# A recurrent attention stage ahead of a routed expert layer: seven idle products of 128 columns in place of fourteen of 64

## The chip, the cores and the metric

The kernel runs on one core of a Trainium2 chip. The metric is the device time of one execution in microseconds; the time of a kernel is the median of its runs. Inputs and outputs are float32.

## What is computed

A gated linear recurrence over 4 x 8 heads, 768 steps and 48 channels makes 3072 rows of 384 numbers; each row then goes to the one of 8 experts whose embedding it is closest to.

```python
for t in range(S):                       # B, H, S, D = 4, 8, 768, 48
    state = alpha[:, :, t, :, None] * state + np.einsum('bhd,bhe->bhde', k[:, :, t], v[:, :, t])
    y[:, :, t] = np.einsum('bhd,bhde->bhe', q[:, :, t], state)
x = y.transpose(0, 2, 1, 3).reshape(B * S, H * D)        # 3072 x 384
logits = xn @ en.T / tau                 # xn, en: rows scaled to length 1
expert_idx = np.argmax(logits, axis=1)
gate_w = probs[np.arange(N), expert_idx] # softmax of the logits
for e in range(E):                       # E = 8, w1: 384 x 1024, w2: 1024 x 384
    mask = expert_idx == e
    h = np.maximum(x[mask] @ w1[e], 0.0)
    out[mask] = gate_w[mask, None] * (h @ w2[e])
```

## The kernel before

The sequence is cut into 24 chunks of 128 steps (six for each of the four batches). The recurrent stage is one loop over the chunks (L719), software-pipelined: in turn s it loads chunk s + 2, decays chunk s, scores chunk s - 1, mixes chunk s - 2 and makes rows of chunk s - 3. Then come the expert layers, which are long chains of products.

At the start `warm(14)` (L713, the function at L684) issues fourteen products of the identity matrix with its own first 64 columns, into a PSUM tile `pw` that nobody reads. They need only `ident`, which POOL makes first. Then `fixed_parts` (L222) fills the constant parts of the buffers on POOL and DVE, `load(0)` (L447) issues the loads of chunk 0 on SP's queue, and `prepare_loads` (L262) issues a few small ones on ACT's. `load(s)` brings the decays `at` in two transfers (L453), the keys `kt` (L454), the queries `qt` (L455), and the values `vt` of chunk s - 1 (L458). There are four buffers of each of the first three and five of the values. Each transfer is made of runs of 192 bytes, 48 numbers.

Within a chunk the order is this. `turned` (L433) transposes the decays on TensorE, four blocks of 128 x 128, into the PSUM tile `pa`; `decays` (L467) scans them backward on DVE into `r` (L480), transposes the keys into `pk`, multiplies both into `kr` (L487), and transposes the queries into `pq`. `queries` (L491) copies `pq` to `qc` on ACT (L496). `decay_queries` (L498) scans `pa` forward on DVE into `a` (L509), and POOL multiplies `qc` and `a` into `qs` (L513). In the next turn `keys_back` (L521) transposes `kr` back into `pkb`, `scores` (L565) multiplies `qs` and `kr` into `sc`, and `update` (L542) makes the next state.

The tiles `pa`, `pk`, `pq` and `pkb`, and a small `p0` of the first chunk (the starts of the decays, which `prepare_first` transposes), take turns in three PSUM buffers (`ps_tr`); `pw` uses the one buffer of `ps_mm`, which later serves `pd` and `px`. Each engine runs its instructions in the order in which the program lists them. `in_turn` keeps TensorE's order that of the code: the idle products, then pa, pk, pq of chunk 0, p0, pkb of chunk 0, then pa of chunk 1. `mm` (L191) and `tr` (L194) are helpers that issue every product and transpose of this stage, so the profile gives those lines (L192, L195) for them, and the tiles tell them apart.

After the last chunks SP fetches the rows that the first expert was sent (`fetch_early`, L176) and the weights (`weights`, L134 on), which need to know which expert comes first.

Of the kernel before, what the change touches and what calls it, by code (L numbers as in the profile page):

```python
# [9 lines left out]
FP32 = mybir.dt.float32  # L10
# [17 lines left out]
def kernel(  # L28
# [16 lines left out]
    P = 128  # L45
# [9 lines left out]
    HALF = P // 2  # L55
# [21 lines left out]
    ident = consts.tile([P, P], FP32)  # L77
# [113 lines left out]
    def mm(*args, **kwargs):  # L191
        last["pe"] = nc.tensor.matmul(*args, **kwargs)  # L192
# [8 lines left out]
    with ExitStack() as c1:  # L201
# [5 lines left out]
        ps_mm = c1.enter_context(tc.tile_pool(name="ps_mm", bufs=1, space=PSUM))  # L207
# [14 lines left out]
        def fixed_parts():  # L222
            for i in range(NBUF):
                nc.gpsimd.memset(at_s[i][:, :, D:DP], 1.0)

                nc.gpsimd.memset(at_s[i][0:1], 0.0)
                nc.vector.memset(kt_s[i][:, :, D:DP], 0.0)
                nc.vector.memset(qt_s[i][:, :, D:DP], 0.0)
                if i == 0:
                    nc.gpsimd.memset(inr, 0.0)  # L230
                    for p in range(NP - 1):
                        nc.gpsimd.memset(inr[:, p * P + P - 1 : (p + 1) * P], 1.0)
                    for j in range(NR):
                        nc.vector.memset(r_s[j][:, NP * P - 1 :], 1.0)
                if i < 2:
                    nc.vector.memset(ini_s[i], 0.0)
            make_upper_triangular(nc, causal[:, 0], val=1.0, diag=True)
            for i in range(NBV):
                nc.vector.memset(vt_s[i][:, :, D:DP], 0.0)
# [443 lines left out]

        def warm(n):  # L684

            pw = ps_mm.tile([P, HALF], FP32, tag="mm", name="pw")
            for _ in range(n):
                mm(pw, lhsT=ident, rhs=ident[:, 0:HALF], start=True, stop=True)

        send = []  # L690
        placed_at = {}
# [18 lines left out]
            return n  # L710

        lead = []
        warm(14)  # L713
        fixed_parts()
        load(0)
        a0 = prepare_loads()
# [712 lines left out]
```

## Time and profile before

| | us |
|---|---|
| median of 3 runs | 405.84 |
| lowest and highest run | 404.31, 406.27 |
| the profiled execution | 416.3 |
| its span, first to last instruction | 414.6 |

| engine | busy, us | share of the span |
|---|---|---|
| PE (TensorE products) | 398.9 | 96% |
| PEld (TensorE weight loads) | 354.6 | 86% |
| DVE (VectorE) | 259.3 | 63% |
| POOL (GpSimd) | 252.7 | 61% |
| ACT (ScalarE) | 205.4 | 50% |

The profile is of one execution, which was slower than the runs that were not profiled. PE's busy time is modelled, since products are pipelined: it says that products were under way, not that TensorE worked at its peak rate. The page cuts the span into 40 slices of some 10.4 us; the recurrent stage takes the first 13, the choice of experts and the first weights two or three more, the experts the rest. TensorE's clock can be granted in full or in part; the record of the clock in the trace begins at 15.14 us, and the views show the time before it as full clock although the instructions there have twice the length of later ones of the same kind.

### The profile page before, as it was taken

What the parts mean: (1) busy time and instruction counts of PE and PEld (TensorE: products, weight loads), DVE (VectorE), ACT (ScalarE), POOL (GpSimd) and SP (SyncE); (2) the same over time, 40 slices, a digit from 0 to 9 for tenths busy, and PEclk for the clock granted to TensorE, in tenths of its full rate; (3) what the DMA queues carried; (4) which work ended last, traced back from release to release, by engine and by line L of the source; (5) the groups of instructions that cost most, each with busy time, mean ns of one, the idle gap of its engine ahead of it and who ended that gap; (6) DMA issues with size and microseconds to landing.
All of it is one profiled execution on the core that took longest, in us unless ns stands there. A gap on an engine that the chain in (4) does not pass through costs nothing. (4 is left out here: it accounts for less than half of the span.)

```text
span 414.6 us, 12189 instructions
## 1 busy us (share of the span) xinstructions
PE 398.9 (96%) x4688; PEld 354.6 (86%) x4688; DVE 259.3 (63%) x655; ACT 205.4 (50%) x516; POOL 252.7 (61%) x344
## 2 busy tenths in 40 slices
PE   8999999999999989999999999999999999899994
PEld 8889989888898768588979979989979979879974
DVE  4999979788889514792583572680582375374640
ACT  3455545554455532653673753662672482492520
POOL 6365687677766434771837939937837755946301
PEclk9999999999999996999999999999999999999998
DMA  9999999998986992495802903703800910100101
GB/s 140 155 166 155 155 185 188 195 193 157 191 174 125 344 371 86 136 344 180 290 16 68 344 19 115 291 19 94 315 20 21 337 50 19 40 2 16 40 16 45
DMA packets 119539, 60.26 MB, mean 145 GB/s; under 512 B 102447, under 2 KB 113976, under 8 KB 119472
## 3 DMA queue, kind: packets, MB, share of 16 engines
q1 hardware_dynamic: 115368, 49.15, 50.2%
q0 software_dynamic: 3728, 10.16, 6.9%
q8 instruction: 44, 0.72, 0.7%
q14 instruction: 23, 0.19, 0.2%
q10 hardware_dynamic: 376, 0.05, 0.1%
HBM read 49.69 MB, written 11.45 MB: 147 GB/s over the span
## 5 line engine op out<-in xcount | busy, mean ns | idle before, releaser
L990 DVE TENSOR_TENSOR hT<-hT,pq 128x384 f32<-128x384 f32 x84 | 45.5, 553 | 50.9 <-PE pq L1098 31.3
L860 POOL DMA_INDIRECT out_dram<-y,sx x25 | 24.6, 983 | 65.9 <-ACT y L995 42.4
L513 POOL TENSOR_TENSOR qs<-qc,a 128x512 f32<-128x512 f32 x24 | 30.6, 1276 | 37.0 <-DVE a L509 15.9
L1098 PE MATMUL pq<-xT_m,w_m 128*128 128x192 f32 x252 | 45.4, 326 | 0.0
L973 PE MATMUL pyo<-w,hT 128*128 128x384 f32 x128 | 42.6, 486 | 0.0
L1098 PEld LDWEIGHTS pq<-xT_m,w_m 128*128 128x128 f32 x252 | 40.8, 190 | 0.0
L973 PEld LDWEIGHTS pyo<-w,hT 128*128 128x128 f32 x128 | 24.0, 190 | 14.8
L312 POOL DMA_INDIRECT xs<-x,dest x24 | 24.2, 1009 | 17.8 <-DVE x L656 10.1
L480 DVE TENSOR_TENSOR_SCAN r<-pa,inr 128x511 f32<-128x511 f32 x24 | 29.2, 1216 | 9.0 <-PE pa L195 8.6
L995 ACT ACTIVATE hT<-hT 128x384 f32<-128x384 f32 x56 | 28.4, 518 | 12.2 <-DVE hT L990 9.6
L1010 POOL TENSOR_TENSOR w_m<-w 128x768 f32<-128x768 f32 x12 | 22.6, 1883 | 17.4 <-PE pq L1195 17.4
L1052 POOL TENSOR_TENSOR w_m<-w,w_m 128x256 f32<-128x256 f32 x42 | 30.1, 729 | 3.8 <-PE pq L1098 2.4
L192 PE MATMUL sc<-qs,kr 64*64 64x128 f32 x768 | 29.4, 273 | 2.1 <-issue 2.1
L509 DVE TENSOR_TENSOR_SCAN a<-pa,ini 128x512 f32<-128x512 f32 x24 | 29.3, 1223 | 1.1
L1195 PE MATMUL pq<-w_m,hT_m 128*128 128x192 f32 x168 | 28.5, 327 | 0.2 <-issue 0.2
L1052 POOL TENSOR_TENSOR w_m<-w 128x256 f32<-128x256 f32 x36 | 26.3, 742 | 3.7 <-PE pq L1098 2.4
L1195 PEld LDWEIGHTS pq<-w_m,hT_m 128*128 128x128 f32 x168 | 27.4, 190 | 0.5 <-issue 0.5
L192 PEld LDWEIGHTS sc<-qs,kr 64*64 64x64 f32 x768 | 22.7, 134 | 4.6 <-issue 4.2
L192 PE MATMUL pyx<-sm,vt 128*64 128x128 f32 x384 | 26.3, 279 | 0.0
L652 ACT COPY lg<-pyx 128x32 f32<-128x32 f32 x24 | 4.4, 185 | 40.8 <-PE px L192 34.7
L192 PEld LDWEIGHTS pyx<-sm,vt 128*64 128x64 f32 x384 | 20.5, 136 | 4.1 <-issue 3.6
L624 ACT COPY ycols<-pyx 128x256 f32<-128x256 f32 x48 | 17.9, 377 | 9.4 <-PE pyx L192 5.9
(230 smaller groups left out, 1003.6 us busy)
## 6 DMA issues: line engine op xcount, KB each, us to landing
w<-in_moe_w_dram SPq DMA_DIRECT2D x12, 1536.0 KB
kt<-in_k_dram SPq DMA_DIRECT2D x24, 192.0 KB
qt<-in_q_dram SPq DMA_DIRECT2D x24, 192.0 KB
vt<-in_v_dram SPq DMA_DIRECT2D x24, 192.0 KB
xg<-xs SPq DMA_DIRECT2D x22, 196.5 KB
at<-in_alpha_dram SPq DMA_DIRECT2D x24, 168.0 KB
w<-in_moe_w_dram SPq DMA_DIRECT2D x6, 512.0 KB
w<-in_moe_w_dram SPq DMA_DIRECT2D x8, 384.0 KB
```

Of the source, the lines that this page charges most:

```text
L192: last["pe"] = nc.tensor.matmul(*args, **kwargs)
L312: ins = nc.gpsimd.indirect_dma_start(out=xs, out_offset=bass.IndirectOffsetOnAxis(ap=rows, axis=0), in_=x, in_offset=None, bounds_check=E ...
L480: nc.vector.tensor_tensor_scan(r[:, L - 2 :: -1], pa[:, L - 1 : 0 : -1], inr[:, L - 2 :: -1], 1.0, ALU.mult, ALU.add,)
L509: d["a_scan"] = by_dve = nc.vector.tensor_tensor_scan(a, pa, ini, 0.0, ALU.mult, ALU.add)
L513: by_pool = nc.gpsimd.tensor_tensor(qs.rearrange("p n t -> p (n t)"), d["qc"], a, ALU.mult)
L860: ins = nc.gpsimd.indirect_dma_start(out=out, out_offset=bass.IndirectOffsetOnAxis(ap=col, axis=0), in_=y, in_offset=None, bounds_check=N - 1,
L973: pe[:] = [nc.tensor.matmul(py, lhsT=hT[:, f], rhs=w2_t[:, f], start=(f == 0), stop=(f == FT - 1),)]
L990: dve[:] = [call(*args, **kwargs)]
L995: act[:] = [call(*args, **kwargs)]
L1052: by(w[to], w[x], w[y], op)
L1098: pe[:] = [nc.tensor.matmul(to[:, f], lhsT=w[left][:, f * P : (f + 1) * P], rhs=x[right], start=start and f == 0, stop=stop, skip_group_ch ...
L1195: pe[:] = [nc.tensor.matmul(to, lhsT=left[:, f], rhs=right[:, f], start=start and f == 0, stop=stop and f == n - 1, skip_group_check=True,)]
```

## The change

`warm` multiplies the identity with all of its 128 columns instead of its first 64, into a tile of 128 columns, and is called with 7 instead of 14. The number of columns that pass through is the same, 896; the number of products, and so of weight loads, is half. TensorE's other instructions, and those of all other engines, keep their number and their order.

```diff
         def warm(n):
 
-            pw = ps_mm.tile([P, HALF], FP32, tag="mm", name="pw")
+            pw = ps_mm.tile([P, P], FP32, tag="mm", name="pw")
             for _ in range(n):
-                mm(pw, lhsT=ident, rhs=ident[:, 0:HALF], start=True, stop=True)
+                mm(pw, lhsT=ident, rhs=ident, start=True, stop=True)
...
         lead = []
-        warm(14)
+        warm(7)
         fixed_parts()
         load(0)
         a0 = prepare_loads()
```

## The prediction, made before the changed kernel was run

> **What bounds the kernel now.** I read the page first (times of the engines, the 40 slices), then the chain of waits, then the timeline of the first 30 us, and the waits in that stretch. The chain of waits follows only the last 32 us, so it can't say what the start is worth; the start has to be read from the timeline.
>
> The page says that the recurrent stage (the first 13 of 40 slices, some 135 us) keeps DVE and the loads busy together:
>
> ```profile
> PE   8999999999999989999999999999999999899994
> DVE  4999979788889514792583572680582375374640
> DMA  9999999998986992495802903703800910100101
> DMA packets 119539, 60.26 MB, mean 145 GB/s; under 512 B 102447, under 2 KB 113976, under 8 KB 119472
> ```
>
> What counts is the first digit of DVE, 4, before a row of 9s: DVE begins late. The timeline (start, duration, engine, line, operation, count, idle time before and its releaser) says why:
>
> ```profile
> 1.55 6.23 PE L192 MATMUL pw<-ident 128*128 128x64 f32 x28 [1.55 <-POOL ident masks.py:199]
> ...
> 7.58 1.06 PE L195 MATMUL pa<-ident,at 128*128 128x128 f32 x4
> ...
> 8.43 1.06 PE L195 MATMUL pk<-ident,kt 128*128 128x128 f32 x4
> 8.75 1.22 DVE L480 TENSOR_TENSOR_SCAN r<-pa,inr 128x511 f32<-128x511 f32 x1 [4.74 <-PE pa L195]
> ...
> 10.07 0.69 DVE L487 TENSOR_TENSOR kr<-pk,r 128x512 f32<-128x512 f32 x1
> ...
> 10.89 1.22 DVE L509 TENSOR_TENSOR_SCAN a<-pa,ini 128x512 f32<-128x512 f32 x1
> ...
> 17.51 0.60 PE L195 MATMUL pa<-ident,at 128*128 128x128 f32 x4
> ```
>
> The first chunk's transposes (pa) stand on PE straight behind the idle products (pw), and DVE waits 4.74 us for pa. Did pa wait for its data? The chunk's decays come in two transfers; the last landing records of their semaphores stand at 3.77 and 4.01 us. So for 3.3 us the data lay there and PE was busy with products nobody reads: the warm-up sets the start, not the load.
>
> From 8.75 us on DVE has hardly a gap: in the waits of the first 30 us the row of r is 5.0 us in two waits, 4.7 of it this first one.
>
> ```profile
> DVE r L480 <- PE pa L195: 5.0, 2, 4.7
> ```
>
> The scan r starts at 8.75, 13.50, 18.15 and 22.59 us: about 4.6 us a chunk. DVE's own work per chunk, from the same rows, is 1.22 (r) + 0.69 (kr) + 0.17 + 1.22 (a) + 0.67 (mask) + 0.41 (state) + 0.27 = 4.65 us. So the stage is paced by DVE, and whatever moves the first r moves the stage, unless the loads stop it.
>
> **What the Trainium skill says.** "TensorE: Matmul & The Clock Gate", Part 1, says that TensorE runs at half clock until about 3.4 us of sustained activity, counted in a free-running window. The trace agrees about the two rates (four transposes: 1.06 us at 7.58, 0.60 at 17.51), but PE is counted busy from 1.55 us and the clock record turns full only at 15.14; products of 64 columns evidently didn't count as enough. Part 4 of the page says that transposes don't count as activity; the trace contradicts it: the 3.4 us before 15.14 held almost nothing else. The section on LDWEIGHTS prices a load by its columns (128 / 1.2 = 107 ns, with no word on f32); here the pitch of a 64-column pass is twice that, so I take the measured pitch. "DMA: Bandwidth & Descriptors", Specifications, wants 512 B per transfer for full rate; here 102447 of 119539 packets are smaller, and the early slices move 140 to 190 GB/s where weight slices reach 344.
>
> **The change, part by part.** *Price of a pass.* An f32 product is two passes: 14 products are the 28 records. Their start-to-start time is (6.23 - 0.42) / 27 = 0.215 us with the first, 0.2134 without it. Does the weight load or the stream of columns set it? Transposes at half clock stream 128 columns behind a load of 128, and have the same pitch: (1.06 - 0.42) / 3 = 0.213. At full clock the start-to-start times in the trace are 323 ns for 384 columns (L973), 163 for 192 (L1098), 112 for 128 (L961): proportional to the columns. So at half clock 64 columns take some 107 ns of stream, 128 some 213, and the load of 128 fills up to 213 beside it. A pass of 128 columns therefore still takes 0.213 us. Bounds: 0.224 (twice 112), and 0.32 if load and stream added up (107 + 213), which the transposes exclude.
>
> *Sum.* 28 passes become 14: 14 x 0.2134 = 2.99 us less PE time (at 0.224: 2.83; at the excluded 0.32: 1.5). PE is free for pa at 7.58 - 2.99 = 4.59 us. The decays landed at 4.01, so pa is still behind the warm-up, by 0.6 us, and gets all of the 2.99. DVE's fills end at 4.0 and hide nothing more.
>
> *What follows in chunk 0.* r starts at 8.75 - 2.99 = 5.76. kr needs pk, whose load landed at 5.60: pk runs 5.65 to 6.71, and r ends at 6.98, so kr keeps the 2.99. pq's load lands at 6.67, so pq gains only 2.4; its copy qc stands behind a square root on ACT that ends at 8.05 and comes at about 8.1 to 8.6. The product qs on POOL waits for the scan a, at about 9.1, so that is hidden. But the backward transposes pkb(0) wait for the PSUM buffer that qc frees: about 8.75 in place of 11.37, 2.6 earlier, and pa(1) stands behind them. At half clock pa(1) then begins at 9.65 and r(1) at 10.8, 2.7 earlier; at full clock r(1) is held by DVE's small product L292, which ends with POOL's qs as before, and keeps 3.0.
>
> *The clock.* With 128 columns the passes are stream without pause. Over the window of 1.48 to 4.90 us (15.14 less three windows of 3.413) I estimate 97% stream where before it was 50%; windows of 67% did not open the gate before, one of 96% did. So the gate probably opens at about 5 us, and at other phases of the window by about 7. That shortens pa by up to 0.3 us. Afterwards PE is waiting for loads in chunk 0 and may fall back for a window or two; then it is as cold as before. I book the clock at nothing, 0 to +0.3 us for r, and -0.3 for the pkb detour.
>
> *What is late next: the loads.* They run by their own queue (SP), filling from 0.8 us on at 160 GB/s, and don't come sooner. Slack between landing and use before: decays 4.0, 4.4, 4.0, 5.1, 4.1 us for chunks 1 to 5; keys 3.8, 3.9, 3.4, 3.2, 3.8; queries 3.4, 3.2, 2.9, 2.6, 3.1, later 3.3 and more, from chunk 10 over 5. A shift of 2.99 takes nearly all of that. Only queries of chunks 3 and 4 come late, by 0.1 and 0.4 us, and their product isn't needed until scan a ends 3 us later. So the loads let 2.6 to 3.0 pass.
>
> *Later.* The expert weights are fetched at 133.4 us and from 134.3, behind scattered rows; 3 us earlier is 131.3, and the last load of the recurrent stage landed at 130.7, so they don't collide. The expert stage follows from these. Nothing is added that anything waits for.
>
> Sum: -2.99, with -3.3 and -2.6 as ends. The profiled execution's 416.3 us (span 414.6, 1.7 around it) would become 413.3, span 411.6. The runs' median is 405.84, 10.5 us under the profiled one; the shift is in PE passes and carries over as it is: **402.8 us**.
>
> **The rivals.**
> A, the load front (chance 0.17): the 3 us are given back to the loads. For it: slack of 2.6 to 4 us in ten chunks, and DMA share over 1 all through. Against it: slack grows to 7 us by chunk 15, so the late chunks are paced by compute. If the unprofiled runs have the loads already at the front, only some 0.5 is left: 405.3.
> B, more than the shift (0.08): the early full clock also shortens chunks 0 and 1, half of some 6 us of PE work at half rate, of which DVE hides most; I give it 1.5 us: 401.3. Against it: DVE was 0.9 busy from 8.75 us on.
> C, slower (0.08): a clock relapse. Running at the load front, PE stands still inside chunks and the gate falls to half. The record of the clock shows one such fall, at 155.1 us, for 6.8 us, after a window with about 30% stream. In the recurrent stage PE streams 90% of a window, so such a fall costs up to 0.9 x 3.4 = 3.1 us more PE time, DVE hiding none once PE is late; two falls cost 6.2, less the 3.0 gained: 409. It decides from two falls on. Against it: a window with 59% stream (141 us) did not bring it down, and stops of a few tenths don't reach that.
> D, the change doesn't do what it says (0.03): passes of 128 columns cost 0.32 and nothing else: 1.5 us less, 404.3.
>
> **How the numbers follow.** The main case has 0.64: 402.8, its own range 402.2 to 404.0. Runs of the kernel before scatter from 404.31 to 406.27, so about 1 us of that goes to each side. Range: 401.0 (B, less scatter) to 405.2 (A nearly whole); C and the rest of A stay out. 0.5%, about what a measurement of this kernel can tell from no change, is 2.0 us: faster is under 403.8. Main case 0.90 of 0.64, B whole, D a third: 0.67. Same: the rest of the main case, A and D: 0.25. Slower: C: 0.08.
>
> **What would show it.** Right: 14 records of pw ending near 4.6 to 4.8 us, pa directly behind them, r at 5.4 to 5.9, idle before r under 2 us, later r starts 2.6 to 3.3 us earlier, the weights' first fetch near 131.3, and a clock record that turns full before 8 us. Wrong: pa waiting for a load; r(5) at 33.9 as before (A); further half-clock stretches before 130 us (C); 0.32 us between passes (D).

## The result, and the profile after

The changed kernel is no faster. Its median was 407.12 us (404.57 to 410.44, 20 runs) against 405.68 for the kernel before (402.92 to 407.99, 20 runs): a ratio of 1.0053, 95% interval 1.0031 to 1.0076. Two later comparisons gave 1.0000 (0.9972 to 1.0027) and 1.0006 (0.9988 to 1.0025), so the small loss of the first did not come back; what stands is that 3 us saved at the start were not seen at the end.

The profiled execution after took 409.06 us, span 407.3, where that of before took 416.3. These two must not be subtracted. The later runs were on three chips: on two of them the kernel before takes about 414 us (before_again to w14x128 on the one, stage_before to after_wlate on the other), on the third about 405 (first_before to light_after). One mark in the traces tells the two kinds apart, two waits of some 3 us on ACT in turns 9 and 13, which are shown further down: all twelve traces from the 414 us chips have them, none of the six from the 405 us chip has. By this mark the profile shown of the kernel before is of the first kind, although the runs beside it took 405.84 us, and the profile after is of the second. More than the change lies between them.

The start is what the prediction said. The timeline of the changed kernel (start, duration, engine, line, operation, count, idle time before and its releaser):

```profile
1.55 3.36 PE L192 MATMUL pw<-ident 128*128 128x128 f32 x14 [1.55 <-POOL ident masks.py:199]
...
4.70 0.66 PE L195 MATMUL pa<-ident,at 128*128 128x128 f32 x4
...
5.47 1.22 DVE L480 TENSOR_TENSOR_SCAN r<-pa,inr 128x511 f32<-128x511 f32 x1 [1.47 <-POOL sel L256]
...
6.26 0.63 PE L195 MATMUL pk<-ident,kt 128*128 128x128 f32 x4 [0.89 <-DMA kt<-in_k_dram]
...
7.23 0.63 PE L195 MATMUL pq<-ident,qt 128*128 128x128 f32 x4 [0.34 <-DMA qt<-in_q_dram]
```

Fourteen passes take 3.36 us where 28 took 6.23; pa follows directly, and r starts at 5.47 instead of 8.75 (pa ended at 5.36; the view names POOL, which ended a small fill in between). But pk and pq, which stood behind products before, now stand behind transfers. That goes on: in the waits of the recurrent stage (8 to 135 us; total, count, longest) there is now a line which the kernel before lacks in its profile altogether.

```profile
PE pq L195 <- DMA qt<-in_q_dram: 4.7, 7, 1.5
```

The page's slices show both. DVE begins with 7 instead of 4, PE with 6 instead of 8.

```profile
PE   6899999989999999989999999989999999999994
DVE  7898988788989436962762762671581484474640
DMA  9999989999999993867306506404701900100101
DMA packets 119539, 60.26 MB, mean 148 GB/s; under 512 B 102447, under 2 KB 113976, under 8 KB 119472
```

The row of DMA says less than it seems to. Of the first 13 slices, which are the recurrent stage, twelve are 9 and one is 8, where the profile of before had 8, 9, 8, 6 in slices ten to thirteen. But the transfers were busy nearly all the time in both (their share from 68 to 129 us is 0.99 against 0.96), the bytes and packets are the same, and the two profiles are of different kinds of chip. Which work waited for transfers is told by the waits.

### The profile page after: what moved, and what is told of

Read it like the earlier page. It is cut to its first block, busy times and chain, and to the rows that moved or that the text cites. A ratio compares the mean times of both kernels' runs of the same rounds, so it can differ in the third digit from the quotient of the medians.

```text
span 407.3 us, 12161 instructions
## 1 busy us (share of the span) xinstructions
PE 387.6 (95%) x4674; PEld 344.0 (84%) x4674; DVE 257.9 (63%) x655; ACT 205.9 (51%) x516; POOL 254.0 (62%) x344
## 5 line engine op out<-in xcount | busy, mean ns | idle before, releaser
L860 POOL DMA_INDIRECT out_dram<-y,sx x25 | 24.6, 982 | 65.5 <-ACT y L995 43.7
L1052 POOL TENSOR_TENSOR w_m<-w 128x256 f32<-128x256 f32 x36 | 27.6, 778 | 4.5 <-PE pq L1098 2.2
L192 PE MATMUL sc<-qs,kr 64*64 64x128 f32 x768 | 25.9, 271 | 0.0
L1010 POOL TENSOR_TENSOR w_m<-w,w_m 128x768 f32<-128x768 f32 x12 | 21.9, 1821 | 0.6
L1202 DVE SCALAR_TENSOR_TENSOR y<-pq,gt,u 128x192 f32<-128x192 f32 x21 | 8.7, 415 | 20.4 <-PE pq L1195 18.8
```

Of the source, the lines that this page charges most:

```text
L860: ins = nc.gpsimd.indirect_dma_start(out=out, out_offset=bass.IndirectOffsetOnAxis(ap=col, axis=0), in_=y, in_offset=None, bounds_check=N - 1,
L1010: by(to, x, y, ALU.subtract)
L1052: by(w[to], w[x], w[y], op)
```

## The experiments

A whole-kernel comparison is good to about 1 us, so the search went by kernels that end early, some of which scatter less, and by the start of DVE's scan r in chunks 0, 5, 12 and 23, read from the timelines; r(5) stands for the scan of chunk 5. Each such start comes from one profiled execution. Differences of medians are between two kernels that ran beside each other on the same chip. The absolute times in the first four expectations are those of the first comparison, which was on a faster chip.

### The change again, and its two parts apart

The kernel before once more, the changed one, and two crossings. In w7x64:

```diff
-        warm(14)
+        warm(7)
```

and in w14x128, beside the wider tile, `warm(14)` is left as it was.

before_again: 

> The kernel before, unchanged, once more. Theory 1 (the profile shown of before was not like its usual runs: its clock opened only at 15.1 us and fell once more at 155 us): this profile has a span near 404 us, its clock record turns full before 10 us, the idle products end before 7.0 us, and there is no half-clock stretch near 155 us. Theory 2 (every run of before is like the one shown, and the changed kernel loses some 4 us elsewhere that it had won at the start): the clock turns full near 15 us, the idle products end at 7.6 to 7.8 us and DVE's first scan starts at 8.75 us. Ratio to before 1.000 within 0.3% under both.

after_again: 

> The changed kernel, once more. Theory 1 (the start is 1 to 2 us earlier than in a usual run of before, and the loads take it back): first scan at 5.4 to 5.8 us, queries used within 0.2 us of their landing in several of the first ten chunks, clock full at 5 to 7 us, median 406 to 408, span 404 to 407. Theory 2: the same start, but a half-clock stretch or a longer expert stage in the profile that the usual runs of before don't have.

w7x64: 

> Seven idle products of 64 columns: as long as the changed kernel's at half clock (14 passes, 3.0 us) but with half of the columns. If the early start is what costs (PE and DVE at the load front), it is as slow as the changed kernel, 406 to 408. If the early full clock is what costs, the clock opens later here (after 8 us) and the time is that of before or under, 404 to 406. If a late clock is what costs, it is the slowest, over 408.

w14x128: 

> Fourteen idle products of 128 columns: as much PE time as before at half clock, with twice the columns, so the clock should open at about 5 us and the products end at about 6.3 us instead of 7.6. If the early start costs, this is between before and the changed kernel, 405.5 to 407. If the early full clock costs, it is as slow as the changed kernel, 407. If neither does, it is as before, 405.7.

On a chip where the kernel before takes 414.23 us, the four took 414.26, 414.05, 414.34 and 413.53 us (ratios 0.9993, 1.0000, 1.0003, 0.9982, each within 0.3% either way). In their traces r(0) starts at 8.76, 5.62, 5.77 and 8.10 us. So r(0) moved by 3.0 to 3.1 us with seven products, wide or narrow, and the time of the whole by at most 1.2 us by the intervals. The passes' form is not the cause: seven narrow ones, which end as early, bring as little.

### How far the gain comes: kernels ended early

stage_before and stage_after end behind the recurrent stage and the choice of experts: no expert weights, no early first layer and no expert layers. early_before and early_after keep the weights of the first two experts and the first layer that runs beside the last chunks. Core of the edits:

```diff
-    with ExitStack() as c3:
...
+    nc.sync.dma_start(out=out[0:P], in_=blank[:, 0:DM])
```

stage_before: 

> The kernel before cut to the recurrent stage and the choice of experts with its scattered rows: the expert weights' loads, the first expert's early layers and all expert layers are left out, and one block of the output is written. Alone it is the reference for the next run. Expected from the profiles of before: about 150 us plus what lies around the span.

stage_after: 

> The same cut with seven idle products of 128 columns. Theory A (the stage itself gives the early start back to the loads): 0 to 1 us under the cut of before. Theory B (the stage keeps some 2 us, as the two profiles of the same chip show at the last chunk, 132.2 against 134.1 us, and something behind it takes them): 1.5 to 2.5 us under the cut of before.

early_before: 

> The kernel before up to the end of the choice of experts, with the weights of the first two experts loaded and the first expert's early first layer; all later expert layers are left out, and one block of the output is written. Reference for the next run; about 175 us.

early_after: 

> The same with seven idle products of 128 columns. Theory A: 0 to 1 us under its reference. Theory B1 (the early first layer takes the gain, waiting for weights that come no sooner): the cut without weights gains 1.5 to 2.5 us, this one 0 to 1. Theory B2 (the gain is lost in the expert layers): this one gains 1.5 to 2.5 us as well.

early_before_2: 

> The cut up to the early first layer, from the kernel before, a second time (its six runs scattered from 174.0 to 179.0 us). Theory B1 (the early first layer and the weights take the gain): the next run is 0 to 1 us under this one. Theory B2 (the gain passes this part and is lost in the expert layers): 1.5 to 2.5 us under it.

early_after_2: 

> The same cut with seven idle products of 128 columns, a second time. B1: 0 to 1 us under its reference, with PE standing still for 1 us or more inside the last chunk's scores, where the kernel before has none; B2: 1.5 to 2.5 us under, and no such stop.

The stage took 163.75 and 161.54 us: some 2 us of the gain are still there when it ends, on a chip of the 414 us kind. With the early layer the two pairs differ by 0.5 and 2.5 us (175.29 and 174.77, 176.47 and 174.00); over all 25 runs it is 1.5 ± 1.4 us. The first pair alone would have said "lost here", the second "kept": one pair of six runs each could not decide it.

In the traces of this kind of chip r(0), r(5), r(12), r(23) start at 8.76, 33.87, 71.36, 134.11 (before_again) and 5.62, 32.03, 69.46, 132.18 (after_again). Of the 3.1 us, 1.3 are given up in the first five chunks (0.9 in the pair of stage kernels), nothing later. In the two pairs with the early layer the lead at r(23) is 1.6 us.

What lies beside the last chunks is the weights' stream. In early_after the last chunk's 32 scores stop before the last two, for 1.33 us in which PE waits for nothing that the profile shows ("issue"); the first product with the weights (phe) comes behind them:

```profile
137.97 1.05 PE L192 MATMUL sc<-qs,kr 64*64 64x128 f32 x29
...
140.35 0.38 PE L192 MATMUL sc<-qs,kr 64*64 64x128 f32 x2 [1.33 <-issue]
140.65 1.56 PE L192 MATMUL phe<-exT,w 128*128 128x256 f32 x6
```

From the first of the scores to the last it is 0.88 us in the kernels that start late (before_again, w14x128, both early_before), and 1.75 to 2.57 in the early ones on these chips (after_again, w7x64, early_after, early_after_2); without any weights (stage_after) it is 0.97. Over all traces with weights the stop goes with one thing: it is there in the five in which the first weights were issued 0.4 to 1.8 us ahead of r(23) (these four and light_after, below), and in none of those in which they were issued at most 0.14 us ahead of it or behind it. In the three pairs here the lead of 1.6 to 1.9 us at r(23) has shrunk to 0.8 (after_again), -0.1 and 0.2 us at the first phe. Without a stop PE is not free of the weights either: in before_again it stands at phe for them, for 0.6 us.

### The weights held back

The first weights' load was made to wait for a small fill of its first column on POOL, placed behind the masks of the last chunk but one (the call of `weights(0)` that stood ahead of it is taken out):

```diff
+            if s == NS - 1:
+                with tc.issue_after(st[NS - 2]["masked"].ins):
+                    nc.gpsimd.memset(w1_s[0][:, 0, 0:1], 0.0)
+                with tc.issue_after(v_last.ins):
+                    weights(0)
```

early_after_wlate: 

> The cut with seven idle products of 128 columns, and the first expert's weights held back by a small fill of their first part behind the mask of chunk 22, so that their stream begins about 1.7 us later and stands to the compute as in the kernel before. If the weights' early stream causes the stop inside the last scores[...], the stop goes, and the cut is 1 to 2 us faster than the one without the hold. If the stop has another cause, it stays, and the time is the same or slower by up to 1 us (weights later).

after_wlate: 

> The whole changed kernel with the same hold on the weights. If the weights' early stream is what took the gain: 1.5 to 2 us under the kernel before. If the gain is lost in the expert layers or in the scatter of runs: within 1 us of the kernel before.

The hold was longer than meant: the weights were issued at 137.38 us, 5 to 6 us later rather than 1.7. The stop in the scores is gone (0.88 us again, in after_wlate too), so it comes with the weights' early stream. But the first product with these weights begins at 140.81, no sooner than in the early kernels without the hold (140.65 and 140.15), because it now waits for them:

```profile
140.81 0.67 PE L192 MATMUL phe<-exT,w 128*128 128x256 f32 x2 [2.81 <-DMA w<-in_moe_w_dram]
```

The rest of the stream is late too: 181.32 us against 174.00 (early_after_2), 420.07 for the whole kernel (1.0156, 1.0102 to 1.0210). As a remedy it fails; as a reading it shows that early weights cost a stop and late ones a wait.

### Past the first expert, on the other kind of chip

first_before and first_after end after the first of the eight experts; after_3 is the changed kernel again; after_hold has a shorter hold, by a fill on DVE ahead of r(23).

```diff
-        for i in range(E):
+        for i in range(1):
...
-        run_rest((E - 1) % NW)
```

first_before: 

> The kernel before, ended after the first of its eight experts (the other seven, and the last scatter of their rows, are left out). Theory 1 (the gain of the start is lost inside the choice and the first expert, where the weights' stream and the late semaphore counts lie): the median of first_before stands within 0.6 us of that of first_after. Theory 2 (the gain of 1.5 to 2.2 us is still there behind the first expert and goes in the seven later ones): first_before is longer by 1.5 us or more. About 205 to 215 us in all.

first_after: 

> The changed kernel, ended after the first of its eight experts in the same way. Theory 1: within 0.6 us of first_before. Theory 2: 1.5 to 2.2 us under it. If it is longer than first_before by over 0.6 us, the first expert gives back more than the start brings.

after_3: 

> The changed kernel once more. If its time against the kernel before depends on the chip (1.0053 in the first comparison, 1.000 in the second), then on a chip where the kernel before takes about 414 us it is again within 0.3% of it; if the two comparisons differ by scatter alone, this one may fall anywhere from 0.998 to 1.005.

after_hold: 

> The changed kernel with the weights of the first two experts held back by a small fill on DVE ahead of the last chunk's r, so that they are issued about as far ahead of r(23) as in the kernel before. If the early weights' stream is what takes the gain away (it stops PE inside the last chunk's scores for 1 to 1.6 us), the stop falls to 0.9 us and the time is 1 to 2 us under after_3, 412 to 413. If the stop only stands in the place of the wait for the same weights, phe begins when it did or later, and the time is that of after_3 within 0.6 us, or up to 2 us more.

This chip was of the 405 us kind (405.10 for the kernel before), like that of the first result. Medians: 191.75 and 190.37 for the two that end after the first expert, or 1.5 ± 1.5 us by all eleven runs, which lies between the two theories and decides neither; 405.40 for after_3 (ratio 1.0006); 404.91 for after_hold (0.9984, 0.9962 to 1.0007). In after_hold the fill came too early to hold anything: the weights were issued at 128.73 us, as in after_3 at 128.83. It tells nothing of the stream, and no version here beats the kernel before.

The traces tell more than the times. The start of r in the four chunks:

| us | r(0) | r(5) | r(12) | r(23) |
|---|---|---|---|---|
| first_before | 8.74 | 34.19 | 70.45 | 130.02 |
| first_after | 5.86 | 31.40 | 67.68 | 129.30 |
| after_3 | 5.85 | 31.80 | 68.15 | 128.82 |
| after_hold | 5.87 | 31.95 | 68.22 | 128.54 |

The lead of first_after is 2.9, 2.8, 2.8 and then 0.7 us: on this kind of chip most of it is lost between chunks 12 and 23. The other two traces of early kernels lose less there, 1.1 and 0.8 us, and more before. The waits of that stretch (68 to 135 us) name a taker, first in first_after, then in first_before (after_3 has 1.3 us in this row, after_hold 0.8):

```profile
PE pq L195 <- DMA qt<-in_q_dram: 2.2, 3, 1.0
```

```profile
PE pq L195 <- DMA qt<-in_q_dram: 0.7, 2, 0.4
```

One such wait in first_after's timeline, in chunk 12, with what stands behind it:

```profile
69.01 0.42 PEld L195 LDWEIGHTS pq<-ident,qt 128*128 128x128 f32 x4 [1.17 <-issue]
69.04 0.63 PE L195 MATMUL pq<-ident,qt 128*128 128x128 f32 x4 [0.97 <-DMA qt<-in_q_dram]
...
70.48 1.06 PE L192 MATMUL sc<-qs,kr 64*64 64x128 f32 x32
...
71.29 0.63 ACT L496 COPY qc<-pq 128x512 f32<-128x512 f32 x1
...
71.99 1.27 POOL L513 TENSOR_TENSOR qs<-qc,a 128x512 f32<-128x512 f32 x1 [2.50 <-ACT qc L496]
```

PE runs its products in the order of the code, so the scores of the chunk before, which need nothing of these queries, come late as well; the turn takes 6.38 us instead of 5.23. Even first_before has no room left at the end: the queries of chunks 19, 21, 22 and 23 land 0.1 us ahead of their first weight load.

Why does the profile of before, on which the prediction rests, show no such wait? There, and in before_again, some turns of the late chunks are longer for another reason: r(9) to r(10) is 6.88 us and r(13) to r(14) 6.90, where first_before has 5.63 and 5.40. The waits of 45 to 135 us in the profile of before:

```profile
ACT lg L652 <- remote: 6.1, 2, 3.1
...
PEld sc L192 <- issue: 3.9, 8, 0.6
...
PE sc L192 <- issue: 2.1, 7, 0.4
```

The first is ACT waiting for small products (px; "remote" says that the view finds nothing on this core that ended the wait): in turn 9 the last of them ends at 55.74 us and ACT goes on at 57.46, where in first_before it goes on 0.05 us behind them. The last px and the wait, first in before, then in first_before:

```profile
55.52 0.22 PE L192 MATMUL px<-sel,ycols 64*64 64x56 f32 x1
57.46 0.18 ACT L652 COPY lg<-pyx 128x32 f32<-128x32 f32 x1 [3.06 <-remote]
```

```profile
55.83 0.22 PE L192 MATMUL px<-sel,ycols 64*64 64x56 f32 x1
56.09 0.19 ACT L652 COPY lg<-pyx 128x32 f32<-128x32 f32 x1 [1.38 <-PE px L192]
```

The other two are stops of PE inside the scores. None of the three is there in first_before or in after_3. The longer turns leave the loads more time: the decays of chunks 12 to 23 lie ready for 7.4 us on average in the profile of before (6.2 in before_again), 2.7 in first_before, 2.0 in first_after (last landing record to the first weight load of their transposes).

### The loads made lighter

To test the loads as the taker, 18 of the 24 loads of v are left out in both kernels:

```diff
-            if s > 0:
+            if 0 < s <= NBV or s == NS:
```

light_before: 

> The kernel before with the loads of v left out for 18 of the 24 chunks (the products of chunks 5 to 22 run on values of v that are already there), so that the recurrent stage's loads carry about a fifth fewer bytes. Theory L (on a chip without late counts from PE the loads pace the later chunks, and give back what the start gains): the queries' transposes stand 1 us or more behind their landing in all chunks from 5 on, and the start of r(23) comes earlier than in first_before (130.0 us) on a chip of the faster kind. Theory K (the loads are not the pace; the gain goes elsewhere): r(23) stands where it did, 130.0 us on such a chip or 134.1 to 134.4 on one where the kernel before takes 414 us.

light_after: 

> The changed kernel with the same 18 loads of v left out. Theory L: with the loads out of the way r(23) starts 2.4 to 3.1 us ahead of that of light_before, where it was 0.7 us between first_before and first_after (2.0 to 2.2 on the slower kind of chip), and the whole time is 1.5 to 3 us under that of light_before. Theory K: r(23) is ahead by no more than before, 0.7 to 1.2 us (2.0 to 2.2 on the slower kind), and the whole times stand within 0.8 us of each other. If r(23) is ahead by over 2.4 us and the whole times are equal all the same, something behind the recurrent stage takes the gain.

| us | r(0) | r(5) | r(12) | r(23) |
|---|---|---|---|---|
| light_before | 8.76 | 33.88 | 70.13 | 129.07 |
| light_after | 5.84 | 31.88 | 68.16 | 127.13 |

From chunk 5 on the lead is now 2.0, 2.0 and 1.94 us: with fewer bytes nothing is lost in the late chunks, where 0.8 to 2.1 was lost with the full loads, and the row of PE waiting for queries is gone from 68 us on in both. The lead is less than the 2.4 that the expectation asked for, since the first five chunks, whose loads were left whole, still take 0.9. The kernel before gains too: r(23) at 129.07 instead of 130.02, most of it behind chunk 19. So on this kind of chip the loads stretch some of the late turns in either kernel, and more of them in the early one. The sizes rest on one trace of each kernel.

The whole times (410.69 and 409.23, six runs each) differ by 1.4 ± 2.1 us, too wide to say more; both are above 405 us. With old values of v the rows go to other experts: these traces hold 128 more products of PE than those of the whole kernels (4816 for 4688, 4802 for 4674), which may be the cause and wasn't tested. But the profile of light_after shows a second taker:

```profile
132.23 1.05 PE L192 MATMUL sc<-qs,kr 64*64 64x128 f32 x29
...
135.73 0.38 PE L192 MATMUL sc<-qs,kr 64*64 64x128 f32 x2 [2.45 <-issue]
136.04 1.56 PE L192 MATMUL phe<-exT,w 128*128 128x256 f32 x6
```

```profile
134.17 1.05 PE L192 MATMUL sc<-qs,kr 64*64 64x128 f32 x31
...
135.16 1.13 PE L192 MATMUL phe<-exT,w 128*128 128x256 f32 x4
```

Above is light_after, below light_before. The early kernel, 1.94 us ahead at r(23), stops 2.45 us within the last scores and begins the first expert's products 0.9 us behind the late one. Its weights were issued from 125.36 us on, 1.8 us ahead of r(23); in light_before from 128.93, 0.1 us ahead.

## Why the prediction was wrong

**Price of a pass: right.** From start to start a pass of 128 columns took 0.213 us, as forecast; the passes end at 4.91 us where they ended at 7.78, 2.87 less for the forecast 2.99, since the first of them took 0.1 us more than its forerunner. And pa begins at 4.70 instead of 7.58, behind them and not behind its load.

**Chunk 0: right in the sum.** r started at 5.47 us, forecast 5.76; the difference is the clock, which the prediction let open at about 5 and booked at nothing. It opened at 4.82 here, and between 4.38 and 6.79 in ten of the eleven traces of kernels that start with seven products of 128 columns (14.21 in the other); in the eight whose products have 64 columns it was 9.56 to 15.78. The forecast relapse came as well, in three of these traces (after_3, stage_after, light_after): half clock from about 8.5 or 9.0 to 12 us, for a few tenths at r(1) or r(2).

**The first five chunks: half right.** "So the loads let 2.6 to 3.0 pass" held in one pair (first_after against first_before, 2.8 at chunk 5) and not in the others (1.5 to 2.4). One of the slacks was misread: for the queries of chunk 3 the prediction has 2.9 us, but the sixteenth and last landing record of that load stands at 21.21 us, 1.6 ahead of its use, so that a shift of 2.99 makes them late by 1.4 and not by 0.1 (in after_again PE waited 1.1 us for just these). And the slack of 2.6 to 4 us was measured for each load by itself, with the queue filling as it did in that execution; moved up by 3 us there is nothing left for a transfer that lands a little later than in the profile. In the traces of the changed kernel PE waited for queries for 0.5 to 2.1 us between 8 and 50 us; in the profile of before it did not.

**The pace: read from too few chunks.** The 4.6 us a chunk, and with it "the stage is paced by DVE", come from the first four scans. Over all 23 turns of the same profile the mean is 5.46 us, and DVE was busy for 87% of the time from 8 to 129 us. So in the late chunks other things than DVE's own work could lengthen a turn, as they did.

**"The runs' median is 405.84, 10.5 us under the profiled one; the shift is in PE passes and carries over as it is": the step that failed.** The saving in the passes was there, but it has to get past two things on its way to the end, and the prediction booked both at next to nothing: the loads at 0 to 0.4 us, the expert stage at nothing.

On the chips of the 414 us kind 1.0 to 1.3 us went by r(23), in the first eight chunks: to the loads for the most part, and in early_after to a clock that stayed at half until 14.21. On the 405 us chip 1.4 to 2.2 us went. How much room the loads leave depends on what fills those 10.5 us. In the profile of before, late releases of ACT and stops in the scores lengthened the turns of the late chunks, and slack grew to 7 us by chunk 15. In executions of the 405 us kind these turns are 1.2 to 1.5 us shorter, the slack of the decays is below 4 us from chunk 12 on, and the loads take 0.8 to 2.1 us there. The 10.5 us were the sign that the slack might not hold, and were taken for a constant.

The prediction named this as its rival A ("If the unprofiled runs have the loads already at the front, only some 0.5 is left: 405.3"), and gave it 0.17 because the slack of the profile spoke against it. Its mechanism was seen on the 405 us chip. That after_3 took 405.40 is in part luck: 0.7 to 1.5 us of the lead were still there at r(23), and the kernel before took 405.10 beside it.

**"so they don't collide. The expert stage follows from these": failed as well.** On the 414 us chips, the kind of the profile, the slack of the late chunks did hold and the lead at r(23) was 1.6 to 2.1 us, but after_again was not faster by more than 1.2. There the loss lies behind the recurrent stage. The weights don't collide with the loads, but with PE: where they come early they stop it inside the last scores, by 0.9 to 2.8 us, in five of the early kernels (on the 405 us chip in light_after alone), and holding them back takes the stop away and puts a wait for the weights in its place.

**Rival C, a clock relapse, was not the cause.** The one in the first chunks costs tenths. Half-clock stretches of 3.4 or 6.8 us behind the recurrent stage occurred in the traces of both kernels, the profile of before among them; on the 414 us chips the early first layer (phe, first to last product) took 21.5 to 24.6 us with one inside it and 19.7 to 21.3 without. On the 405 us chip no trace has one there, and the gain was missing all the same.

**What stays open.** The first comparison's loss of 0.5% did not recur, and no cause of it is shown. In the profile after, the loads ran late: the decays of chunk 19 landed at 106.13 us, against 103.04 in after_3, and r(23) began at 131.50 against 128.82. For a kernel at the load front that is a loss, but there is no profile of the kernel before from that comparison that could show whether its loads ran late too. Behind r(23) a lead of 0.7 to 1.5 us (405 us kind) or 1.6 to 2.1 us (414 us kind) goes on to nothing that whole-kernel runs can tell. The stop takes part of it where it occurs, the scatter of the first expert is another candidate, and the share of each wasn't separated; the kernels that end after the early layer or after the first expert still differ by 1.5 us, give or take 1.4 or 1.5.

## What to carry to other kernels

When a profiled execution is longer than the runs by more than they scatter (here 2.6%), find out which waits fill the difference before reading slack from it: slack is what those waits give to the other engines, and it goes with them. Removing work ahead of a loop that is fed by one queue of transfers is worth only what the transfers let pass over the whole loop, not in the first chunks. And a stream that is issued behind the moved work moves along with it, and meets other work there.

## What the runs showed of the hardware

- TensorE's clock: transposes count as work for it, since from 11.73 to 14.97 us in the profile of before PE ran nothing else, and the clock opened at 15.14. Products of 64 columns in f32 did not open it: in the eight kernels that start with them it opened at 9.56 to 15.78 us, behind their end; in ten of eleven that start with seven products of 128 columns it opened by 6.79. The stretches of the record are 3.41 us or multiples, and their phase differs from one execution to the next.
- A stream of weights can go with a stop of PE where it waits for no semaphore that the profile shows: 1.33 us in early_after, 2.45 in light_after, both before the last two of 32 scores, and none without the weights or with them held back. That PE's own instructions come late then is a guess; a transfer of the instructions' queue stands near each stop (16 KB from 137.97 us in early_after, from 133.35 in light_after), and no run tested it.
- In all traces of the 414 us kind ACT waits for px for some 3 us in two turns of the recurrent stage, and in the one shown it goes on 1.7 us behind the last of these products; in those of the 405 us kind it does not. In the first expert's first full layer of before_again DVE went on 5.9 us behind the transposes that it waited for, and ACT then made four results in a burst. That layer, from its first product to the first of the next one, took 11.63 and 12.29 us in before_again and after_again (in after_again with a half-clock stretch inside it), and 6.67 in the other traces that have it, two of the same chip among them.
